# Clustered attention and a SoLU layer on one core: paired x transposes, row placements without mutual waits, and a new written order

## The chip, the cores and the metric

The kernel runs on one core of one Trainium2 chip. The core has five engines that run their own instruction streams and meet at semaphores: TensorE (PE; its weight loads are listed apart as PEld), VectorE (DVE), ScalarE (ACT), GpSimd (POOL) and SyncE (SP), which here does nothing but issue DMAs. The metric is the device time of one execution in microseconds (us), lower is better. "Span" is the time from the first to the last instruction of a profiled execution.

## What is computed

Two parts, one after the other. The first is attention restricted to clusters: each query and each key is assigned to the nearest of 16 centroids of its head, and a query sees only keys of its own cluster. The second is a feed-forward layer with a SoLU activation (h times softmax of h) and a layer norm, over rows of 512 that hold all 8 heads of a token.

```
batch, n_heads, seq, head_dim = 4, 8, 768, 64        # n_clusters = 16
q_assign = argmax(q_n . c_n)                         # q_n, k_n, c_n: rows of unit length
k_assign = argmax(k_n . c_n)
scores = where(q_assign == k_assign, q . k / sqrt(64), -1e9)
attn   = softmax(scores) @ v
x      = attn.transpose(0, 2, 1, 3).reshape(3072, 512)
h      = x @ w_in                                    # 512 x 1024
solu   = h * softmax(h)
ln     = (solu - mean) / sqrt(var + 1e-6) * g_ln     # over the 1024
out    = ln @ w_out                                  # 1024 x 512, float32
```

## The kernel before

**Attention.** The work goes by batch b (0 to 3) and pair p of heads (0 to 3). Queries and keys of a pair are loaded (`ld`, four DMAs of 96 KB for each of q and k in batches 1 to 3), turned so that the head dimension lies on the partitions (`xt` on VectorE; in batch 0 `tp` on TensorE and a copy `xa`), and cast to bf16 into a tile `qk` (`ca`). For each token the products with the centroids are made (`cl`, TensorE), transposed back (`tb`), reduced to their maximum (`mx`), compared with it into a one-hot row (`oh`), and turned again (`ot`), all on VectorE. These one-hot rows are then placed below the casted rows of the `qk` tile (`pl`, line 450), for queries and keys (i = 0, 1) and for the first and second half of the columns (part = 0, 1): four placements for a pair, by VectorE, GpSimd or a DMA of SyncE. `bl` zeroes some rows. One matmul over the casted rows and the one-hot rows together (`S`, line 535) gives the score plus a large bias where the clusters agree; the exponential (`E`, ScalarE, line 541) takes the bias off again. The exponentials are the weights of the matmuls with v (`V`, line 558; v is loaded by `lv` and cast by `cv`), whose last column is the sum for the softmax. `N` (lines 570 and 583, VectorE) divides by it and writes x in bf16.

Scores go by units; a group of units shares one accumulator bank, so that the first `V` of a group waits for `N` of the group before. In batches 0 to 2 the units of the last head pair are grouped by two token blocks: blocks 2s and 2s+1 of both heads end in one `N`. In batch 3 the heads 4 to 7 are done one token block at a time.

**Feed-forward.** It goes by token blocks f of 128 rows (24 of them, six per batch). `tx` (lines 600 to 604) turns x of a block by a transposing DMA into a buffer `xT`, of which there are four. `h` (line 634) are four steps of two matmuls into two of three banks; `hm` the maximum (640), `ex` the exponential (646), `u` the product (651); `tu` (656) turns u by a DMA; `bn` and `ag` the statistics; `at` and `al` the scale factor on GpSimd; `y` (692) the second matmul, four steps of two; `sc` (700 on ScalarE, 702 on VectorE) the scaling; `ou` (712) the store. The last blocks' `tx` and `tu` are done by TensorE instead.

**The order.** The program's class `Weave` holds, for each of the five engines, a written order: a text of kinds with counts ("ld4 lv si ld7 ...") that is expanded, kind by kind, into the operations in the order in which they were added. `AWAY` lists the operations that run on another engine than their first choice. `add` declares each operation with its estimated cost, the operations that it needs, and those that it must come after. From this the program computes start times with a model and emits the instructions in that order; on the chip each engine runs its own stream in the written order, and waits at semaphores that the framework derives from the tiles each instruction reads and writes. An operation that must wait holds up all that follow it on its engine; for SyncE that is every load, transpose, placement and store behind it.

Operations are named by kind and indices: `tx6` is the x transpose of block 6, `ld3.3.1` the load of the keys of pair 3 in batch 3 (its fourth part), `pl2.3.0.1` the placement of the second half of the query rows of pair 3 in batch 2.

The dependence of two placements on each other comes from the framework: they write different columns of the same rows of one `qk` tile, and where they run on different engines, the later one waits for the earlier.

Of the kernel before, what the change touches and what calls it, by code (L numbers as in the profile page):

```python
# [10 lines left out]
F32 = mybir.dt.float32  # L11
# [11 lines left out]
class Weave:  # L23
# [6 lines left out]
        ld4 lv si ld7 lg ld lv ld8 lo3 lv ld4 lo lv ld4 li ld li2 ld5 li ld3 tx ld3 lv tx ld9 tx tu  # L30
        lv ld tx ld3 tx tu ld2 tx lv ld4 pl ld4 lv ld4 lv ld4 ou lv tu2 ld4 tx ld2 ou ld tx2 ld2 tu2
        ou ld tx ld7 tx lv ld4 ou2 tu ld2 pl ld3 tu ld2 lv ld tx lv pl ld pl ou ld2 lv ld2 tu pl tu
        ld2 pl ou tx ld3 tx pl2 ld tx ld ou tx2 lv tu2 tx lv ou tu ou pl ou pl2 ou tu2 tx ou tu tx2
        tu2 ou2 tx tu tx ou tu ou2 tu2 ou6
    """
    ORDER["POOL"] = """
        po z2 ca2 pl ca bl cv ca pl cv pl bl pl2 z ca z pl ca2 pl2 ca2 pl cv2 ca2 pl2 sg ca2 bl cv
        pl cv pl3 ca2 bl cv wi2 pl2 bl wi pl wi pl ca3 pl2 bl pl cv ca z ca3 pl ca cv at2 ca cv pl2
        ca2 pl2 bl al cv2 ca al at pl bl at pl2 cv2 ca6 at al cv pl cv pl3 at cv ca2 bl al2 pl2 ca3
        pl2 ca bl at ca pl al ca4 pl2 al cv2 ca2 bl at ca pl2 cv at al cv bl al ca2 pl at bl pl ca  # L40
        cv at2 cv ca pl al pl2 al2 bl cv pl4 at ca cv at cv al at3 al3 at2 al at al at al at al at
        al at al3
    """
    ORDER["PE"] = """
        tp cp tp2 cl tp cl tp2 S3 tp2 S tp2 S2 cl S3 tp2 S V2 S V tp S cl V2 S V S tp gt S3 tp S4 V
        S V2 S5 V2 S V tp S3 cl S2 V2 S2 V S V3 S5 V3 S V S3 V2 S4 me S3 V3 S V2 S V S3 cl S V S2 V
        S V2 S2 V2 S5 V4 S3 cl S2 V2 S2 V2 S3 V2 S h S h S3 h2 S V S2 V cl S2 h S V4 h V S V S2 h S2
        h V S2 V2 S cl V S h S V2 S h y S3 h S h V2 S V S h S y2 S3 V h y V S2 V S h2 S2 V4 S V S2 V
        S h y2 h S2 y S2 V2 S V S y S V S V S h2 V S2 h2 cl S3 V2 S V4 S3 h2 S3 cl S V4 S3 y3 V S3
        V3 S y S2 h3 V S V2 S3 V y S h S2 y S2 V S y2 S V4 h2 S V S2 cl S h V h S2 V2 S y S2 y V3 S3  # L50
        h y2 h S2 h2 S h V S2 h y3 V S V y S V S V2 S y2 S y V2 S3 V2 h S y S2 V S V h S cl S3 V2 h
        V S cl V S2 h S2 cl S2 V2 S2 h S h2 S V3 S2 V2 y S2 y V y2 S2 h V2 S V S V S y S2 V2 S2 h V
        h S V S2 y S2 y2 S V h2 S2 V3 S cl S3 h2 S V2 S V2 S2 V2 h cl S3 h3 S y V y3 S V S V S h S h
        V2 S V S h S2 h S V2 h S V y S2 y V y S h S y V S2 V S h2 V h S2 y S2 y S y V y V4 S2 h2 S2
        h y S V h V3 y S y S2 y S h V S3 V3 h2 S V h S2 y V y3 S2 h V S V h2 S y3 S y S h S h y V2
        h2 S3 h S V2 y3 S2 V2 h3 V S V y3 h y S3 h y h2 y3 h2 S y4 S h2 V4 y3 ptx y h2 y h2 y3 ptu2
        y4 ptu2 y8
    """
    ORDER["DVE"] = """
        cn cb ca xa tb mx oh ot pl2 tb pl mx oh xa3 ot pl xa pl tb mx oh ot tb N bl xa xt gk mx oh  # L60
        ot su2 xa2 N su cv ca su2 tb N su ca2 mx su2 oh ot N xt ce xt N ce2 tb mx oh N ot ce xt N
        ce4 N tb mx oh ot xt2 hm cv N tb u xt N xt hm mx bn tb u oh N ot bn hm mx oh xt u ot N ag bn
        hm sc bn2 N ag u xt bn xt2 hm bn N u tb N mx ag oh hm ot tb N bn xt u bn N mx xt bn ag cv oh
        N ot ag hm xt bn2 u ag ca N tb mx xt hm ca bn N u oh xt ot hm xt2 u ca N bn2 ag bn3 ca xt N
        hm tb mx oh ot tb u xt ag mx N bn oh tb cv2 ot ag hm mx N sc u N oh xt bn hm ot N bn xt sc u
        N bn bl tb hm xt ag bn u tb N hm mx2 oh u ot oh N sc hm bn ag bn ag bn cv ot u N hm bn2 ca
        bn u bl ag N hm N bn u N sc hm bn2 ag2 u bn ag hm N bn u bn2 hm N u bn2 ag2 hm N bn u bn2 ag
        hm sc bn ag u ag bn hm N tx u bn ag bn hm sc bn u ag tu2 bn2 ag
    """
    ORDER["ACT"] = """  # L70
        wa xa2 ca2 xa2 ca E ca E4 xa E4 xa2 E19 xa E58 ex E10 ex E11 ex E9 ex E9 sc E5 ex E11 ex E8
        sc E10 ex E2 sc E9 ex E5 sc E ex E3 sc E8 sc E6 ex E8 ca E8 ex E12 ex E11 ex E3 ca2 E3 ex
        E10 ex E4 sc E6 ex E sc E6 ex E9 ex E3 sc E2 ex sc E5 ex E4 sc E ex sc E2 ex E3 sc ex sc ex
        sc tu2 sc2
# [3 lines left out]
        ca0.0.0.0.0 ca0.0.0.1.1 ca3.1.0.1 ca3.3.0.0 ca3.3.0.1 tu23.1 xa0.0.0.0 xa0.1.0.0 xa0.2.0.1  # L78
        xa0.2.1.0 xa0.2.1.1 xa0.3.1.1
    """.split(), "ACT"))  # L80
    AWAY.update(dict.fromkeys("""
        bl0.1 bl3.1 bl3.3 ca0.0.1.0.0 ca0.3.0.0 ca0.3.1.0 ca1.0.0.0 ca2.2.0.0 ca2.3.0.1 ca3.0.0.0
        ca3.0.0.1 ca3.3.1.1 cv0.1.0 cv1.0.1 cv2.0.1 cv2.3.1 cv3.0.0 cv3.2.1 pl0.0.0.0.1 pl0.0.0.1.1
        pl0.0.1.1.1 sc0 sc12 sc17 sc20 sc7 sc8 sc9 tu22.0
    """.split(), "DVE"))
    AWAY.update(dict.fromkeys("""
        ca0.0.1.0.1 pl0.0.0.1.0 pl0.0.1.1.0 pl0.1.0.0 pl0.1.0.1 pl0.1.1.0 pl0.1.1.1 pl0.2.0.0
        pl0.2.0.1 pl0.2.1.0 pl0.2.1.1 pl0.3.0.0 pl0.3.0.1 pl0.3.1.0 pl0.3.1.1 pl1.0.0.0 pl1.0.0.1
        pl1.0.1.0 pl1.0.1.1 pl1.1.0.0 pl1.1.0.1 pl1.1.1.0 pl1.1.1.1 pl1.2.0.0 pl1.2.0.1 pl1.2.1.0
        pl1.2.1.1 pl1.3.0.0 pl1.3.0.1 pl1.3.1.1 pl2.0.0.0 pl2.0.0.1 pl2.0.1.0 pl2.0.1.1 pl2.1.0.0  # L90
        pl2.1.0.1 pl2.1.1.0 pl2.1.1.1 pl2.2.0.0 pl2.2.0.1 pl2.2.1.1 pl2.3.0.1 pl2.3.1.1 pl3.0.0.0
        pl3.0.0.1 pl3.1.0.0 pl3.1.0.1 pl3.2.0.0 pl3.2.0.1 pl3.2.1.0 pl3.3.1.0 pl3.3.1.1
# [79 lines left out]
def kernel(  # L172
# [276 lines left out]

    def place(b, p, hf, i, part, e):  # L450

        n = asg[b, p, hf, "n"]
        r = slice((2 * i + part) * NB, (2 * i + part + 1) * NB)
        lo = (hf or 0) * HALF + part * n
        dst = side(b, p, i, slice(0, 2), slice(lo, lo + n))[D:D + NB]
        src = asg[b, p, hf, "oht"][r, :n]
        if e == "SP":
            nc.sync.dma_start(out=dst, in_=src.unsqueeze(1).to_broadcast([NB, 2, n]))
        else:
            VEC[e].tensor_copy(dst.bitcast(F32), src.bitcast(F32).unsqueeze(1)  # L460
                               .to_broadcast([NB, 2, n // 2]))
# [137 lines left out]

    def turn_x(f):  # L600
        b, su = divmod(f, n_t)
        xTs[f] = mo.tile([P, n_dc, P], BF16, name="xT", bufs=4)
        nc.sync.dma_start_transpose(out=xTs[f][:],
                                    in_=xs[b][:, su].rearrange("p h d -> p (h d)"))

    def turn_x_pe(f):
        b, su = divmod(f, n_t)
        xTs[f] = mo.tile([P, n_dc, P], BF16, name="xT", bufs=4)
# [5 lines left out]
    def keep_x(f):  # L614
        nc.vector.tensor_copy(xTs[f][:], ff[f, "xp"][:])
# [313 lines left out]
    for g, ns in enumerate(GROUPS):  # L929
# [14 lines left out]
        if b >= 2:  # L944
            nd += [f"tx{(b - 2) * n_t + s2}" for s2 in range(n_t)]
# [15 lines left out]
    for f in range(n_f):  # L961
# [5 lines left out]
        prev = s  # L967
    for f in range(n_f):
        s = pos[f] - 8 * (f == n_f - 1)
        b, su = divmod(f, n_t)  # L970
        gs = sorted({group_of[where[b, h, su]] for h in range(H)})
        nd = [f"N{g2}" for g2 in gs]
        if f >= 4:
            nd.append(f"h{f - 4}.1.1")
        if f"tx{f}" in turns:
# [122 lines left out]
```

## Time and profile before

| what | value |
|---|---|
| median of 3 runs | 243.21 us (242.08 to 243.49) |
| the profiled execution | 242.2 us, of which the span is 240.3 us |
| mean granted TensorE clock | 0.997 |
| DMA | 39.13 MB in 134158 packets, mean 163 GB/s |
| DMAs issued by SyncE, by kind | 96 loads of 96 KB after batch 0, 23 x transposes, 22 u transposes, 24 stores, 11 placements, 16 loads of v |

The profile lists, for each engine, its busy time and its instructions in order of time; where an engine sat idle, the brackets behind a row give the idle time just before it and what ended it. Several instructions of one line that follow each other are merged into one row with their count. "SPq" rows are DMA issues of SyncE; their duration is the time that SyncE spent on issuing. A tile view gives the shortest, median and longest duration of the instructions that write or read a tile.

### The profile page before, as it was taken

What the parts mean: (1) busy time and instruction counts of PE and PEld (TensorE: products, weight loads), DVE (VectorE), ACT (ScalarE), POOL (GpSimd) and SP (SyncE); (2) the same over time, 40 slices, a digit from 0 to 9 for tenths busy, and PEclk for the clock granted to TensorE, in tenths of its full rate; (3) what the DMA queues carried; (4) which work ended last, traced back from release to release, by engine and by line L of the source; (5) the groups of instructions that cost most, each with busy time, mean ns of one, the idle gap of its engine ahead of it and who ended that gap; (6) DMA issues with size and microseconds to landing.
All of it is one profiled execution on the core that took longest, in us unless ns stands there. A gap on an engine that the chain in (4) does not pass through costs nothing.

```text
span 240.3 us, 6552 instructions
## 1 busy us (share of the span) xinstructions
PE 220.1 (92%) x2380; PEld 146.3 (61%) x2380; DVE 201.6 (84%) x359; ACT 196.2 (82%) x378; POOL 125.0 (52%) x234
## 2 busy tenths in 40 slices
PE   2999898999999989899996999897999999999983
PEld 1555575576767757576664666664676776665541
DVE  3885999999899969969959999678898778899880
ACT  3597998999899989978977999786999988885442
POOL 2446699899547778749184555242049204033130
PEclk9999999999999999999999999999999999999998
DMA  6999889979898989989889959757991523747522
GB/s 160 263 240 247 209 210 257 197 114 190 143 177 171 154 190 212 146 170 164 135 213 170 163 141 163 160 93 142 210 170 64 131 56 81 195 91 209 141 86 89
DMA packets 134158, 39.13 MB, mean 163 GB/s; under 512 B 124712, under 2 KB 129520, under 8 KB 134128
## 3 DMA queue, kind: packets, MB, share of 16 engines
q1 hardware_dynamic: 132528, 38.34, 77.6%
q10 hardware_dynamic: 1600, 0.39, 0.7%
q8 instruction: 18, 0.29, 0.5%
q14 instruction: 12, 0.10, 0.1%
HBM read 23.11 MB, written 6.29 MB: 122 GB/s over the span
## 4 chain that ended last, share of the span: by engine, by line
PE 55%; DVE 15%; DMA 14%; SPq 6%; issue 4%; ACT 4%; POOL 0%; DVEq 0%; ACTq 0%; POOLq 0%
PE sps L535 16%; PE yps L692 13%; PE hreg L634 13%; PE ops L558 9%; DMA uT<-u 6%; DMA raw<-in_q_dram 3%; SPq L358 3%; PE csc L415 3%; ACT e L541 3%; DVE nmax L640 2%; DVE w_sum L513 2%; DMA vf<-in_v_dram 2%; SPq L378 2%; DMA raw<-in_k_dram 2%; DVE xt L386 2%
## 5 line engine op out<-in xcount | busy, mean ns | idle before, releaser
L541 ACT ACTIVATE e<-sps 128x512 bf16<-128x512 f32 (+1 forms) x294 | 152.1, 600 | 18.7 <-PE sps L535 17.0
L535 PE MATMUL sps<-qk 80*128 80x256 bf16 (+5 forms) x636 | 97.3, 264 | 2.2 <-ACT e L541 0.4
L535 PEld LDWEIGHTS <-qk 96*128 96x128 bf16 (+1 forms) x636 | 60.6, 121 | 32.1 <-issue 13.6
L558 PEld LDWEIGHTS <-e 128*128 128x128 bf16 x1152 | 51.0, 97 | 13.5 <-issue 4.9
L558 PE MATMUL ops<-v,e 128*128 128x65 bf16 x1152 | 55.3, 193 | 1.9 <-DVE x L583 1.3
L634 PE MATMUL hreg<-w_in_sb,xT 128*128 128x512 bf16 x192 | 52.9, 379 | 1.1 <-DMA xT<-x 1.0
L692 PE MATMUL yps<-w_out_c,uT 128*128 128x512 bf16 x184 | 48.9, 379 | 4.3 <-DMA uT<-u 3.6
L460 POOL COPY qk<-oht 32x384 f32<-32x384 f32 (+1 forms) x52 | 27.9, 536 | 25.9 <-DVE oht L448 19.4
L646 ACT ACTIVATE e_sb<-hreg,nmax 128x1024 bf16<-128x1024 f32 x24 | 26.8, 1116 | 9.6 <-DVE nmax L640 9.5
L640 DVE TENSOR_REDUCE nmax<-hreg 128x1 f32<-128x1024 f32 x24 | 29.0, 1207 | 4.6 <-PE hreg L634 4.4
L662 DVE BATCH_NORM_STATS2 bs<-u 128x6 f32<-128x512 bf16 x48 | 31.4, 673 | 0.0
L678 POOL TENSOR_SCALAR esq<-es,mv 128x1 f32<-128x1 f32 x24 | 9.1, 378 | 41.7 <-DVE mv L666 39.3
L386 DVE STREAM_TRANSPOSE xt<-raw 128x768 f32<-128x768 f32 x24 | 23.3, 969 | 8.5 <-DMA raw<-in_q_dram 3.7
L651 DVE TENSOR_TENSOR u<-e_sb,hreg 128x1024 bf16<-128x1024 bf16 x24 | 28.9, 1202 | 1.4 <-ACT e_sb L646 1.0
L692 PEld LDWEIGHTS <-uT 128*128 128x128 bf16 x192 | 17.2, 97 | 17.8 <-DMA uT<-u 4.3
L406 POOL TENSOR_SCALAR qk<-xt 64x768 bf16<-64x768 f32 (+1 forms) x29 | 24.6, 848 | 2.2 <-DVE xt L386 0.4
L634 PEld LDWEIGHTS <-xT 128*128 128x128 bf16 x192 | 17.0, 97 | 9.9 <-DMA xT<-x 1.3
L404 POOL CAST qk<-xt 64x768 bf16<-64x768 f32 (+1 forms) x23 | 19.7, 856 | 5.7 <-DVE xt L372 4.7
L583 DVE TENSOR_TENSOR x<-ops,den 128x384 bf16<-128x384 f32 (+1 forms) x37 | 18.6, 504 | 1.3
L474 POOL CAST v<-vf 128x384 bf16<-128x384 f32 x26 | 14.2, 553 | 8.0 <-DMA vf<-in_v_dram 7.3
L415 PE MATMUL csc<-xt,c_bd 128*32 128x384 f32 (+1 forms) x136 | 16.6, 501 | 1.4 <-DVE xt L386 1.3
L700 ACT ACTIVATE y<-yps,alpha 128x512 f32<-128x512 f32 x16 | 11.2, 701 | 4.8 <-PE yps L692 1.7
(69 smaller groups left out, 159.3 us busy)
## 6 DMA issues: line engine op xcount, KB each, us to landing
vf<-in_v_dram SPq DMA_DIRECT2D x16, 384.0 KB, 4.5
out_dram<-y SPq DMA_DIRECT2D x24, 256.0 KB, 2.3
raw<-in_q_dram SPq DMA_DIRECT2D x50, 96.0 KB, 3.4
raw<-in_k_dram SPq DMA_DIRECT2D x50, 96.0 KB, 3.2
w_g<-in_moe_w_out_dram SPq DMA_DIRECT2D x4, 512.0 KB, 5.7
w_st<-in_moe_w_in_dram SPq DMA_DIRECT2D x4, 512.0 KB, 5.1
raw<-in_q_dram SPq DMA_DIRECT2D x6, 192.0 KB, 4.0
raw<-in_k_dram SPq DMA_DIRECT2D x6, 192.0 KB, 4.4
```

Source lines behind the costliest of these rows:

```text
L386: nc.vector.transpose(xt[:], raws[b, p, i][:].rearrange("p j c -> p (j c)"))
L406: VEC[e].tensor_scalar(dst, xt[r, cols], scalar1=inv_C, scalar2=1.0, op0=Alu.mult, op1=Alu.mult)
L460: VEC[e].tensor_copy(dst.bitcast(F32), src.bitcast(F32).unsqueeze(1) .to_broadcast([NB, 2, n // 2]))
L535: nc.tensor.matmul(sps_[n, k][:, c0:c0 + w], side(b, h // 2, 1, h % 2, keys)[r], side(b, h // 2, 0, h % 2, slice(s0 * P, s0 * P + w))[r])
L541: nc.scalar.activation(es[n, k][:, :w], sps_[n, k][:, :w], Act.Exp, scale=exp_scale, bias=-exp_scale)
L558: nc.tensor.matmul(opss[g][:, s, :VW], es[n, k][:, c0:c0 + P], v1[slot(b, h // 2)][:, h % 2, kt, :VW], start=(kt == 0), stop=(kt == n_t - 1))
L634: uses(nc.tensor.matmul(hreg[:, at(f, f2)[1], :], xTs[f][:, dc, :], w_in_sb[:, dc, f2 * FF2:(f2 + 1) * FF2], start=(dc == 0), stop=(dc == ...
L640: uses(nc.vector.tensor_reduce(ff[f, "nmax"][:], pair_of(f), axis=AXY, op=Alu.max, negate=True), *both(f))
L646: uses(nc.scalar.activation(ff[f, "e"][:], pair_of(f), Act.Exp, bias=ff[f, "nmax"][:], accum_out=ff[f, "esum"][:]), *both(f))
L651: uses(nc.vector.tensor_tensor(ff[f, "u"][:], ff[f, "e"][:], pair_of(f), op=Alu.mult), *both(f))
L662: nc.vector.bn_stats(ff[f, "bs"][:, f2, :], ff[f, "u"][:, f2, :])
L692: ins = nc.tensor.matmul(ff[f, "y"], ff[f, "uT"][:, at(f, f2)[0] * (n_fc // 2) + c, :], w_out_c[:, fc, :], start=(fc == 0), stop=(fc == n_ ...
```

## The change

Four things change.

1. `turn_x` takes two token blocks with one DMA in batches 0 to 2 (f below 18): blocks 2s and 2s+1 go as one transpose of 128 by 1024 into a buffer for two blocks, of which there are three. In batch 3 it stays one block at a time, in a buffer of the same size. Nine of the 23 transposing DMAs of x disappear, and the `h` steps of both blocks wait for the one DMA.
2. `place` declares to the framework that two placements into the same tile side, if they are on different engines, do not depend on each other ("other columns").
3. The planner gets further needs (`reader`): steps of block f that reuse a small buffer name the step of block f - 4 that reads it. They emit no instruction.
4. The five written orders and the lists in `AWAY` are new. By the lists, 66 operations change their engine; among them two copies `xa`, some casts, zeroings and scalings go to VectorE, and eight placements instead of 11 are DMAs of SyncE.

```
     def place(b, p, hf, i, part, e):
...
         if e == "SP":
-            nc.sync.dma_start(out=dst, in_=src.unsqueeze(1).to_broadcast([NB, 2, n]))
+            ins = nc.sync.dma_start(out=dst, in_=src.unsqueeze(1).to_broadcast([NB, 2, n]))
         else:
-            VEC[e].tensor_copy(dst.bitcast(F32), src.bitcast(F32).unsqueeze(1)
-                               .to_broadcast([NB, 2, n // 2]))
+            ins = VEC[e].tensor_copy(dst.bitcast(F32), src.bitcast(F32).unsqueeze(1)
+                                     .to_broadcast([NB, 2, n // 2]))
+        for other in placed.get((b, p, hf, i), []):
+            if other.ins.engine != ins.ins.engine:
+                tc.declare_no_dep(ins.ins, other.ins, reason="other columns")
+        placed.setdefault((b, p, hf, i), []).append(ins)
...
+    def turned(f):
+        return list(range(f - f % 2, f - f % 2 + 2)) if f < (B - 1) * n_t else [f]
+
+    def take_x(f):
+        fs = turned(f)
+        xT = mo.tile([P, 2, n_dc, P], BF16, name="xT", bufs=3)
+        for j, f1 in enumerate(fs):
+            xTs[f1] = xT[:, j]
+        return xT[:, :len(fs)].rearrange("p s c t -> p (s c) t")
+
     def turn_x(f):
         b, su = divmod(f, n_t)
-        xTs[f] = mo.tile([P, n_dc, P], BF16, name="xT", bufs=4)
-        nc.sync.dma_start_transpose(out=xTs[f][:],
-                                    in_=xs[b][:, su].rearrange("p h d -> p (h d)"))
+        nc.sync.dma_start_transpose(out=take_x(f), in_=xs[b][:, su:su + len(turned(f))]
+                                    .rearrange("p s h d -> p (s h d)"))
...
+    def reader(kind, f):
+        return [f"{kind}{f - 4}"] if f >= 4 else []
...
-            add(f"tx{f}", "SP", 1.28, s, (lambda e, f=f: turn_x(f)), nd,
-                [f"tx{f - 1}"] if f else [], move=0.75, lag=(0.1, 0.7))
...
+                add(f"tx{f}", "SP", 1.28, s, (lambda e, f=f: turn_x(f)), nd,
+                    [f"tx{x_turns[-1]}"] if x_turns else [], move=0.65 * len(fs), lag=(0.1, 0.7))
...
-                nd = [f"tx{f}"] + [f"wi{dc}" for dc in range(n_dc)]
+                nd = [f"tx{fs[0]}"] + [f"wi{dc}" for dc in range(n_dc)]
...
-                [f"u{f}"], [f"bn{f}.0"] if f2 else [])
-        add(f"ag{f}", "DVE", 0.13, s + 8, (lambda e, f=f: f_aggr(f)), [f"bn{f}.0", f"bn{f}.1"])
...
+                [f"u{f}"] + reader("ag", f), [f"bn{f}.0"] if f2 else [])
+        add(f"ag{f}", "DVE", 0.13, s + 8, (lambda e, f=f: f_aggr(f)),
+            [f"bn{f}.0", f"bn{f}.1"] + reader("al", f))
```

The part of SyncE's order that the prediction speaks of, before (first) and after, with the operations' names, around the transpose of block 6 and on to the last load of batch 3:

```
ld2.3.0.0 ld2.3.0.1 ld2.3.0.2 tx6 ld2.3.0 ld2.3.1.0 ou1 ld2.3.1.1 tx7 tx8 ld2.3.1.2 ld2.3.1 tu4 tu5
ou2 ld3.0.0.0 tx9 ld3.0.0.1 ld3.0.0.2 ld3.0.0 ld3.0.1.0 ld3.0.1.1 ld3.0.1.2 ld3.0.1 tx10 lv2.2
ld3.1.0.0 ld3.1.0.1 ld3.1.0.2 ld3.1.0 ou3 ou4 tu6 ld3.1.1.0 ld3.1.1.1 pl2.2.1.0 ld3.1.1.2 ld3.1.1
ld3.2.0.0 tu7 ld3.2.0.1 ld3.2.0.2 lv2.3 ld3.2.0 tx11 lv3.0 pl2.3.1.0 ld3.2.1.0 pl2.3.0.0 ou5
ld3.2.1.1 ld3.2.1.2 lv3.1 ld3.2.1 ld3.3.0.0 tu8 pl3.0.1.0 tu9 ld3.3.0.1 ld3.3.0.2 pl3.0.1.1 ou6 tx12
ld3.3.0 ld3.3.1.0 ld3.3.1.1 tx13 pl3.1.1.0 pl3.1.1.1 ld3.3.1.2 tx14 ld3.3.1

ou1 ld2.3.0.0 ld2.3.0.1 tx6 tu3 ld2.3.0.2 ld2.3.0 ld2.3.1.0 tu4 tu5 tx8 ou2 ld2.3.1.1 ld2.3.1.2
ld2.3.1 ld3.0.0.0 ld3.0.0.1 ld3.0.0.2 lv2.2 tu6 ld3.0.0 ou3 ld3.0.1.0 ld3.0.1.1 ld3.0.1.2 ld3.0.1
pl2.2.1.1 tx10 lv2.3 ld3.1.0.0 ld3.1.0.1 pl2.2.0.0 ld3.1.0.2 ld3.1.0 ld3.1.1.0 ld3.1.1.1 ou4
ld3.1.1.2 ld3.1.1 ld3.2.0.0 ld3.2.0.1 ld3.2.0.2 ld3.2.0 ld3.2.1.0 tu7 lv3.0 lv3.1 ou5 ou6 ld3.2.1.1
ld3.2.1.2 ld3.2.1 ld3.3.0.0 ld3.3.0.1 ld3.3.0.2 tu8 ld3.3.0 lv3.2 ld3.3.1.0 ld3.3.1.1 ld3.3.1.2 tx12
ld3.3.1
```

124 lines of the change are left out of this document (65 added, 59 removed).

## The prediction

> **What bounds the kernel now.** I read the page's busy shares first, then the busy time of each engine in stretches of 20 us, then the idle time of TensorE in order of time, and last SyncE's issues just ahead of each idle piece.
>
> ```profile
> span 240.3 us, 6552 instructions
> PE 220.1 (92%) x2380; PEld 146.3 (61%) x2380; DVE 201.6 (84%) x359; ACT 196.2 (82%) x378; POOL 125.0 (52%) x234
> ```
> ```profile
> 0.00:20.00 20.00, 14.83 (x123) 8.83 (x124) 12.90 (x40) 11.43 (x26) 8.84 (x27) 1.00 0.93 216
> 20.00:40.00 20.00, 17.96 (x195) 11.61 (x194) 18.44 (x33) 18.20 (x40) 15.85 (x20) 1.00 0.89 225
> 40.00:60.00 20.00, 19.19 (x252) 13.42 (x251) 19.34 (x35) 19.30 (x37) 18.16 (x29) 1.00 0.93 186
> 60.00:80.00 20.00, 19.55 (x246) 14.69 (x245) 18.93 (x30) 18.59 (x37) 11.82 (x22) 1.00 0.94 164
> 80.00:100.00 20.00, 19.20 (x226) 13.45 (x224) 17.72 (x32) 18.72 (x38) 15.76 (x30) 1.00 1.03 179
> 180.00:200.00 20.00, 20.00 (x248) 14.25 (x247) 15.95 (x28) 17.96 (x35) 7.92 (x19) 1.00 0.39 93
> ```
>
> The columns of the second fence are the stretch, its length, then PE, PEld, DVE, ACT and POOL busy, the granted clock, the DMA share and GB/s. TensorE is the bound: from 180 to 200 us it has no idle time at all. So only TensorE's idle time ahead of that can be won. From 20 to 80 us VectorE has almost none either (1.56, 0.66 and 1.07 us, 3.29 us in all); ScalarE is close behind. The DMA engines are at 0.89 to 1.03 up to 100 us.
>
> The idle pieces of TensorE between 86 and 170 us are these:
>
> ```profile
> 90.20 0.54 PE L558 MATMUL ops<-v,e 128*128 128x65 bf16 x12 [0.80 <-DVE x L583]
> 101.73 1.47 PE L634 MATMUL hreg<-w_in_sb,xT 128*128 128x512 bf16 x6 [1.04 <-DMA xT<-x]
> 128.06 1.04 PE L692 MATMUL yps<-w_out_c,uT 128*128 128x512 bf16 x4 [2.44 <-DMA uT<-u]
> 150.84 0.61 PE L692 MATMUL yps<-w_out_c,uT 128*128 128x512 bf16 x2 [1.11 <-DMA uT<-u]
> 166.34 0.84 PE L415 MATMUL csc<-xt,c_bd 128*32 128x384 f32 x4 [1.28 <-DVE xt L386]
> ```
>
> In brackets stand the idle time and what ended it. The last four, 5.87 us together, belong by the written order to h6, y6, y8 and cl3.3, and all four wait for something that SyncE issued. SyncE's own queue tells why it came late:
>
> ```profile
> L378 SPq DMA_DIRECT2D raw<-in_q_dram x48: 336/526/3358, 15.6 to 155.2; - x48
> ```
> ```profile
> 98.92 1.20 SPq L603 DMA_TRANSPOSE xT<-x  x1
> 118.79 4.68 SPq L378 DMA_DIRECT2D raw<-in_q_dram  x4
> 123.57 0.94 SPq L712 DMA_DIRECT2D out_dram<-y  x2
> 124.62 1.29 SPq L656 DMA_TRANSPOSE uT<-u  x1
> 137.60 0.62 SPq L458 DMA_DIRECT2D qk<-oht  x1
> 141.15 0.59 SPq L458 DMA_DIRECT2D qk<-oht  x1
> 145.26 3.82 SPq L656 DMA_TRANSPOSE uT<-u  x1
> 157.00 2.39 SPq L603 DMA_TRANSPOSE xT<-x  x1
> 162.76 0.59 SPq L378 DMA_DIRECT2D raw<-in_k_dram  x1
> ```
> ```profile
> 96.06 0.18 DVE L570 RECIPROCAL den<-ops 128x4 f32<-128x4 f32 x1 [0.31 <-PE ops L558]
> 96.27 0.42 DVE L583 TENSOR_TENSOR x<-ops,den 128x256 bf16<-128x256 f32 x1
> 140.06 1.06 POOL L460 COPY qk<-oht 32x384 f32<-32x384 f32 x2 [4.04 <-DMA qk<-oht]
> ```
>
> The first row gives the shortest, median and longest issue of a load in ns. In the others the columns are start, duration, engine and line. The x of block 6 was complete at 96.69 (the normalising step), but its transpose was issued at 98.92, behind two loads. The transpose tu6 stands behind four loads and the stores ou3 and ou4 and issues at 124.62; y6 follows it. A row placement at 137.60 holds GpSimd for 4.04 us, and those GpSimd copies in turn hold the next placement to 141.15: halves of one tile waiting for each other, with tu8 behind them. The last load, ld3.3.1 at 162.76, stands behind the transposes tx12 to tx14 and was what cl3.3 waited for.
>
> **The change part by part.** *One transpose for two blocks.* Nine of 23 x transposes go. The nearest row for the double one is uT, whose 128 by 1024 bf16 is the pair's shape exactly:
>
> ```profile
> L603 SPq DMA_TRANSPOSE xT<-x x23: 1189/1258/2551, 50.0 to 214.1; - x23
> DMA to landing us min/median/max: 2.4/3.0/5.1
> L656 SPq DMA_TRANSPOSE uT<-u x22: 1232/1277/3824, 63.4 to 221.6; - x22
> DMA to landing us min/median/max: 3.0/3.3/6.4
> ```
>
> SyncE is freed of 9 x 1.258 = 11.3 us of issuing, less 9 x 0.02 us for the larger one, spread over the first three batches, from 50 us on; the landing of the first block of a pair comes 0.3 us later. Bytes moved are the same. A pair could have to wait for its second block, but here doesn't: in batches 0 to 2 the last head pair is normalised for blocks 2s and 2s+1 in one step, so both become ready together. Three buffers of two blocks hold no less than four of one. On TensorE's path itself: nothing; the worth is in what SyncE issues earlier.
>
> *Placements without waiting.* This takes away waits like the 4.04 us on GpSimd and the one that ended at 141.15. No instruction goes. Neither is on TensorE's path by itself; the gain is already in y8 below. At worst it is nothing.
>
> *The planner's "reader" edges* add no instruction and no wait on the chip: they only constrain how the order is built.
>
> *The new order.* I expanded both written orders by operation and compared places. The work between two places I count in TensorE time at these rates:
>
> ```profile
> 183.40 0.44 PE sps L535 x4
> 186.57 0.75 PE ops L558 x24
> 187.79 0.86 PE hreg L634 x4
> ```
>
> For h6: tx6 has one load less straight ahead, and by the median issue times it comes some 5 us of issuing earlier in SyncE's order, so that it waits only for its own x. From the last value matmul it needs to h6 lie 4.5 us of TensorE work in both orders; it needs normalising (96.06 to 96.69 here, with the hop some 0.7 us) and 3.3 us to land, 4.0 us: gone. For y6: tu6 now stands ahead of ou3, ou4 and most of the ld3.0 and all ld3.1 loads, with 24 us of TensorE work between y2 (the last store ahead of it is ou2) and y6: gone. For y8: tu8 has only ou6 ahead, 19 us before y8, and both pl2.3 placements of the second part are on GpSimd: gone. For cl3.3: ld3.3.1 is passed by one transpose only, not three, and stands right behind tx12, whose x is ready some 6 us of TensorE work before h12: gone. So 5.87 us are removed. The 0.80 us at 90.20 I leave as it is.
>
> What does SyncE's new order hold up instead? tu3 now stands behind tx6, which blocks the queue until its x is ready. From there to y3 lie 13 pairs of score matmuls, 30 value matmuls and 16 matmuls of the two layers: 26 x 0.11 + 30 x 0.031 + 16 x 0.215 = 7.2 us; needed are 0.7 + 1.26 + 3.3 = 5.3 us, so it is hidden with 1.9 us to spare; without that cover it costs what is missing. I find no worse place, but the present order let four SyncE stalls through as well. New stalls are between 0 and the same 5.87 us; I take one as large as the largest there is, 2.44 us, since SyncE has 11.3 us more room.
>
> *Work moved between engines.* To the end of batch 1, VectorE gets a net two turned-token copies, two half casts, two zeroings and one output scaling; full casts and v casts that come and go cancel, and two short placements that leave it I don't count.
>
> ```profile
> L372 DVE COPY xt<-hreg 128x384 f32<-128x384 f32 x8 | 4.2, 548 | 0.1
> 7.07 0.35 DVE L406 TENSOR_SCALAR qk<-xt 64x384 bf16<-64x384 f32 x1 [0.69 <-ACT xt L372]
> L465 DVE MEMSET qk<- 16x384 f32 x3 | 1.1, 378 | 0.9 <-DMA qk<-oht 0.7
> L702 DVE TENSOR_SCALAR y<-yps,alpha 128x512 f32<-128x512 f32 x7 | 5.2, 741 | 0.4
> ```
>
> That is 2 x 0.548 + 2 x 0.35 + 2 x 0.378 + 0.741 = 3.3 us. The casts and one copy lie in the first 20 us, where VectorE has 7.1 us idle; one copy, the zeroings and the scaling, 2.0 us, come later, against 3.29 us of idle time. A loss is between 0 and 3.3 us, and I take a third of the later ones, 0.7. In the start, the first turned copy moves to VectorE and the second key transpose goes ahead of the centroids' one, which attacks the 0.69 us that VectorE waits for ScalarE's copy: a gain of 0 to 0.69, taken as 0.4. On the other side the two copies leave ScalarE, which is nearly full at 20 to 60 us; that stays uncounted.
>
> *Sum:* -5.87 - 0.4 + 2.44 + 0.7 = -3.1 us. The profiled execution took 242.2 us (its span 240.3 and 1.9 around it) and would become 239.1; the median of the runs, 243.2, lies 1.0 higher, so 240.1 us.
>
> **Rivals.** *VectorE becomes the bound* (slower). The added 3.3 us meet 3.29 us of idle time from 20 to 80 us. If the early idle time can't take them, because it consists of waits for data, each normalising step up to about 85 us comes up to 3.3 us later; value matmuls need it for their bank, as the 0.80 us row shows, and x transposes block SyncE for as long, so that the old stalls come back in other places. Then 243.2 + 3.3 - 0.4 = 246.1 us. It decides from the point where the work ahead of a normalising step grows by more than VectorE's idle time before it. For it: 19.34 of 20 us busy. Against: counted over the written order, the work ahead of u6 (the product at about 110 us) grows by only some 0.3 us, since other steps move behind it, so it would be a passing delay. Chance 0.15.
>
> *The transfers bind, not their issue* (no change). With the DMA share at 0.89 to 1.03, an earlier issue only queues longer; the four loads at 118.79 took 4.68 us to issue where the median is 0.526 each, which speaks for it. Against: the waits behind stores, placements and unready x aren't transfers. Only the start is gained: 242.8 us. Chance 0.17.
>
> *VectorE's casts hold up GpSimd* (within 1%).
>
> ```profile
> L460 POOL COPY qk<-oht x52: 343/503/1191, 9.9 to 183.2; 32x384 f32<-32x384 f32 x49, 32x192 f32<-32x192 f32 x3
> L460 POOL COPY qk<-oht x11: 498/503/507, 39.6 to 57.3; 32x384 f32<-32x384 f32 x11
> ```
>
> The first row is the whole span, the second 40 to 60 us. In batches 0 and 1 VectorE has nine casts and zeroings more and five fewer, net four; if each stretches one GpSimd copy from 503 to 1191 ns, GpSimd loses 2.8 us where it is busy for 18.16 of 20, and the forecast becomes 242.9 us. Against: in just that stretch all eleven copies took 498 to 507 ns. Chance 0.05. [...]
>
> *All is won*, without new stalls and with ScalarE's relief: under 236.9 (243.2 - 5.87 - 0.4). Chance 0.05.
>
> **How the numbers follow.** The forecast, the removed stalls less one new one, has 0.58 and runs from 236.9 (nothing given back) to 242.9; I put 0.48 of it below 240.8 and 0.10 above. One per cent, 2.4 us, is about what a measurement of this kernel can tell from no change. Faster: 0.48 + 0.05 = 0.53. Within 1%: 0.10 + 0.17 + 0.05 = 0.32. Slower: 0.15. The range goes from 236.9 to 245.5; below lies 0.05, above most of the slower case, 0.13.
>
> **What would show it.** Right: nine x transposes fewer, each pair landing in about 3.3 us; no idle TensorE at h6, y6, y8 and cl3.3; no GpSimd wait on a placement's DMA for copies; at most some 3 us of new idle pieces. Wrong: value matmuls waiting on the normalising step between 25 and 85 us (VectorE), loads and transposes that land later after issue while SyncE waits less (transfers), or GpSimd copies well over 503 ns.

## The result, and the profile after

| kernel | median (lowest to highest) | ratio to before, 95% interval |
|---|---|---|
| before | 243.35 us (242.08 to 246.94, 4 runs) | |
| after | 232.62 us (232.27 to 232.70, 4 runs) | 0.957 [0.953, 0.961] |

Each ratio, here and below, leaves out the runs in a slower state of the chip, while the medians take them in, so a quotient of two medians can differ from the ratio.

The change is worth 4.3%, more than the range that was forecast allowed. The profiled execution of after took 232.3 us, with a span of 230.3 us, 10.0 us less than the span of before.

The page of after, span and busy time of each engine:

```profile
span 230.3 us, 6548 instructions
PE 217.0 (94%) x2380; PEld 146.8 (64%) x2380; DVE 204.7 (89%) x363; ACT 194.2 (84%) x375; POOL 123.6 (54%) x236
```

Next the busy time in stretches, with the columns of the prediction: after from 0 to 100 us, and the middle part, 60 to 180 us, as one stretch; then that middle stretch of before.

```profile
0.00:20.00 20.00, 16.23 (x127) 10.03 (x128) 15.49 (x43) 12.48 (x28) 8.43 (x24) 1.00 0.93 228
20.00:40.00 20.00, 17.21 (x206) 11.37 (x204) 19.42 (x36) 17.32 (x37) 16.29 (x26) 1.00 1.00 223
40.00:60.00 20.00, 18.40 (x242) 12.39 (x241) 18.65 (x32) 18.78 (x38) 14.62 (x24) 1.00 0.89 185
60.00:80.00 20.00, 20.00 (x250) 15.34 (x247) 19.26 (x32) 19.37 (x38) 12.46 (x22) 1.00 1.03 182
80.00:100.00 20.00, 19.81 (x237) 14.32 (x236) 19.79 (x36) 19.33 (x39) 14.64 (x28) 1.00 0.84 181
...
60.00:180.00 120.00, 119.81 (x1387) 85.86 (x1384) 111.38 (x188) 114.25 (x219) 72.86 (x135) 1.00 0.86 167
```
```profile
60.00:180.00 120.00, 112.50 (x1270) 78.22 (x1269) 104.74 (x178) 105.77 (x203) 63.38 (x116) 1.00 0.90 165
```

The first busy figure of a row is TensorE's. Between 60 and 180 us its idle time falls from 7.50 us (120 less 112.50) to 0.19. Before 60 us nothing is won: busy for 51.98 us there before (the three rows in the prediction), 51.84 after. After 180 us the idle time is 0.3 us more. The remaining part of the 10 us is a fall of TensorE's own busy time, 220.1 to 217.0, which the section on the prediction comes back to.

All of after's idle pieces of TensorE from 15 to 190 us that the timeline names:

```profile
33.03 0.55 PE L564 MATMUL ops<-v,e 128*128 128x65 bf16 x12 [1.32 <-DVE x L589]
38.05 0.35 PE L564 MATMUL ops<-v,e 128*128 128x65 bf16 x6 [0.58 <-DVE xt L386]
48.37 0.55 PE L564 MATMUL ops<-v,e 128*128 128x65 bf16 x12 [1.01 <-DVE x L589]
90.78 1.04 PE L650 MATMUL hreg<-w_in_sb,xT 128*128 128x512 bf16 x4 [0.19 <-DVE u L667]
```

None is ended by a DMA any more. The paired transposes, from the tile view of `xT`, and SyncE's queue around the steps that were late before:

```profile
L619 SPq DMA_TRANSPOSE xT<-x x14: 1190/1270/2688, 50.4 to 204.2; - x14
...
DMA to landing us min/median/max: 2.4/3.3/4.9
```
```profile
109.97 1.24 SPq L672 DMA_TRANSPOSE uT<-u  x1
...
126.00 3.79 SPq L378 DMA_DIRECT2D raw<-in_q_dram  x4
...
140.32 1.31 SPq L672 DMA_TRANSPOSE uT<-u  x1
...
145.25 1.67 SPq L619 DMA_TRANSPOSE xT<-x  x1
146.97 0.57 SPq L378 DMA_DIRECT2D raw<-in_k_dram  x1
```

The first row takes in the five single transposes of batch 3. The nine pairs alone took SyncE 1.287 us each (median), against 1.255 for the 18 single ones in whose place they stand, so a pair costs SyncE what a single one cost; it lands after 3.7 us instead of 3.0. `tu6` goes out at 109.97 instead of 124.62, `tu8` at 140.32 instead of 145.26, and the last load of all, `ld3.3.1`, at 146.97 instead of 162.76, 15.8 us earlier. Four loads still take 3.79 us to issue at 126.00, but no named idle piece of TensorE is ended by them. No GpSimd copy waits for a placement's DMA any more, as the prediction said.

### The profile page after: what moved, and what is told of

Its sections match the earlier page's. It is cut to its first block, busy times and chain, and to the rows that moved or that the text cites. A ratio compares the mean times of both kernels' runs of the same rounds, so it can differ in the third digit from the quotient of the medians.

```text
span 230.3 us, 6548 instructions
## 1 busy us (share of the span) xinstructions
PE 217.0 (94%) x2380; PEld 146.8 (64%) x2380; DVE 204.7 (89%) x363; ACT 194.2 (84%) x375; POOL 123.6 (54%) x236
## 4 chain that ended last, share of the span: by engine, by line
PE 72%; DVE 15%; DMA 4%; issue 3%; POOL 2%; ACT 2%; SPq 1%; DVEq 0%; ACTq 0%; POOLq 0%
PE sps L541 21%; PE hreg L650 16%; PE yps L708 16%; PE ops L564 12%; PE csc L415 4%; PE hreg L365 2%; DVE xt L386 2%; DMA w_st<-in_moe_w_in_dram 2%; DVE w_sum L519 2%; DMA vf<-in_v_dram 1%; DVE nmax L656 1%; DVE oh L442 1%; ACT e L547 1%; POOL qk L462 1%; DVE bs L678 1%
## 5 line engine op out<-in xcount | busy, mean ns | idle before, releaser
L462 POOL COPY qk<-oht 32x384 f32<-32x384 f32 (+1 forms) x57 | 30.9, 541 | 39.0 <-DVE oht L448 27.3
L694 POOL TENSOR_SCALAR esq<-es,mv 128x1 f32<-128x1 f32 x24 | 8.2, 344 | 39.3 <-DVE mv L682 22.1
L406 POOL TENSOR_SCALAR qk<-xt 64x768 bf16<-64x768 f32 x28 | 23.5, 840 | 5.8 <-DVE xt L386 3.9
L386 DVE STREAM_TRANSPOSE xt<-raw 128x768 f32<-128x768 f32 x24 | 22.6, 954 | 0.0
L404 POOL CAST qk<-xt 64x768 bf16<-64x768 f32 (+1 forms) x22 | 18.4, 834 | 1.0
L415 PE MATMUL csc<-xt,c_bd 128*32 128x384 f32 (+1 forms) x136 | 16.0, 502 | 0.1
L716 ACT ACTIVATE y<-yps,alpha 128x512 f32<-128x512 f32 x15 | 10.4, 693 | 5.5 <-PE yps L708 2.7
```

Source lines behind the costliest of these rows:

```text
L386: nc.vector.transpose(xt[:], raws[b, p, i][:].rearrange("p j c -> p (j c)"))
L415: nc.tensor.matmul(csc[c * NB:(c + 1) * NB, :n], c_bd[:, p, :], xts[b, p, i][:, lo + part * n:lo + (part + 1) * n], tile_position=(0, c * NB))
L462: ins = VEC[e].tensor_copy(dst.bitcast(F32), src.bitcast(F32).unsqueeze(1) .to_broadcast([NB, 2, n // 2]))
```

## The experiments

The theories: **A**, the new written order carries the gain; **B**, the pairing does, because SyncE issues one thing after another and everything behind nine issues comes earlier; **D**, the placements' waits do; **E**, the pair's buffers give the x transposes more room; **F**, a pair is cheaper as a transfer than two single ones, whoever issues it. Where an expectation names another letter, it says there what is meant.

All results, each ratio against the kernel before on the same chip (its median beside it). The rows come from three chips: `after_old_sync_order` and the three with `v_on_gpsimd` from a second, the last two rows from a third. The kernel before moved by up to 1 us on one and the same chip (240.95 to 242.02), so differences of under 1% between rows with different values of "before" say little.

| run | median us | before us | ratio, 95% interval |
|---|---|---|---|
| pairs_in_old_order | 237.67 | 242.02 | 0.981 [0.972, 0.990] |
| no_waits_in_old_order | 238.88 | 242.02 | 0.988 [0.980, 0.997] |
| both_in_old_order | 233.95 | 241.44 | 0.973 [0.967, 0.979] |
| new_order_alone | 239.28 | 241.44 | 0.994 [0.990, 0.999] |
| unpaired | 238.77 | 241.44 | 0.992 [0.989, 0.996] |
| placements_wait | 232.18 | 241.44 | 0.966 [0.957, 0.975] |
| six_buffers | 242.32 | 242.02 | 1.001 [0.996, 1.006] |
| tiny_loads | 235.89 | 242.02 | 0.974 [0.968, 0.981] |
| before_v_on_gpsimd | 244.42 | 241.65 | 1.014 [1.005, 1.023] |
| unpaired_v_on_gpsimd | 241.86 | 241.65 | none |
| after_v_on_gpsimd | 237.76 | 241.65 | 0.986 [0.977, 0.995] |
| after_old_sync_order | 242.86 | 241.65 | 1.007 [1.003, 1.012] |
| sync_pause | 238.07 | 240.95 | 0.990 [0.985, 0.994] |
| before_fewer_v | 232.25 | 240.95 | 0.968 [0.961, 0.975] |
| unpaired_fewer_v | 234.63 | 240.95 | 0.978 [0.970, 0.985] |
| changed_again | 231.83 | 240.95 | 0.967 [0.959, 0.975] |
| after_fewer_v | 234.31 | 241.96 | 0.966 [0.956, 0.975] |
| new_sync_order_old_rest | 256.07 | 241.96 | 1.054 [1.043, 1.066] |

`unpaired_v_on_gpsimd` has no ratio, and nothing below rests on it.

### Which part of the change

**One code change each, in the old order.** `pairs_in_old_order` takes only the pairing, and strikes the second transpose of each pair from SyncE's list; `no_waits_in_old_order` takes only the declaration in `place`.

```
-        ... si ld3 tx ld3 lv tx ld9 tx tu lv ld tx ...
+        ... si ld3 tx ld3 lv ld9 tx tu lv ld4 ...
```

> The kernel before with one change: pairs of x blocks turned by one DMA (three buffers of two), the odd x transposes struck out of the order, placements waiting as before. B (each transpose fewer moves all behind it in SyncE's full queue forward): 233 to 235 us. D (the missing waits of the placements did it in the run with both code changes): 238 us or more.

> The kernel before with one change: placements don't wait for each other; x turned singly, four buffers, old orders. B: 240 to 243 us, as before within 1%. D: 234 to 238 us.

**Both code changes in the old order, and the new order without either.** The second one has single transposes, six `xT` buffers and the waits.

> The code changes alone (pairs, no mutual waits of placements), in the five orders of the kernel before, with the nine odd x transposes struck out. Theory A (the places in SyncE's written order make the gain): the loads and u transposes stand behind the same steps as before, so little is won: 240 to 243 us. Theory B (nine transposes fewer free SyncE and the DMA engines): most of the gain is here: 233 to 236 us. Theory C (the orders of the compute engines and the moves between engines make it): 241 to 243 us, as A.

> The five new orders and the new AWAY lists alone: two single x transposes stand where the pair stood (buffers for six blocks as in the changed kernel), placements wait for each other. A: 233 to 235 us, since two issues in one place hold SyncE only 1.26 us longer. B: 239 to 243 us. C: 233 to 235 us, as A.

The two code changes without any new order already give 2.7%, and the new order without them 0.6%. A falls. One at a time in the old order, the pairing gives 1.9% and the missing waits 1.2%, which add up to a little more than the 2.7% of both together. So D has a share there. Both single runs, 237.67 and 238.88 us, came out between the ranges of B and of D, since neither expected that the gain would be divided.

**One code change taken out of the changed kernel.** `unpaired` has two single transposes where a pair was, and six buffers of one block; `placements_wait` has only the declaration removed.

```
     def turned(f):
-        return list(range(f - f % 2, f - f % 2 + 2)) if f < (B - 1) * n_t else [f]
+        return [f]
...
-        for other in placed.get((b, p, hf, i), []):
-            if other.ins.engine != ins.ins.engine:
-                tc.declare_no_dep(ins.ins, other.ins, reason="other columns")
-        placed.setdefault((b, p, hf, i), []).append(ins)
```

> The changed kernel with two single x transposes in the place of each pair, all else kept. A and C: 232.5 to 234.5 us. B: 237 us or more.

> The changed kernel without the declaration, so that placements of one tile side on different engines wait for each other again. A, B and C: 232.5 to 233.5 us, since in the new order the halves seldom meet in time. A rival D, that the missing waits make the gain (in the kernel before one such chain held SyncE for some 2.3 us ahead of tu8, and GpSimd for 4.0): 235 us or more, with idle TensorE again behind SyncE between 140 and 155 us.

Without the pairing most of the gain is gone: 238.77 against 232.18 for its companion on the same chip, 6.6 us. The waits of the placements cost nothing that shows in the new order. So the same 1.2% that the missing waits give in the old order is covered by the rest of the change. The longer idle pieces of TensorE in `unpaired` after 60 us:

```profile
64.58 0.60 PE L653 MATMUL hreg<-w_in_sb,xT 128*128 128x512 bf16 x2 [0.68 <-DMA xT<-x]
82.94 0.61 PE L711 MATMUL yps<-w_out_c,uT 128*128 128x512 bf16 x2 [1.16 <-DMA uT<-u]
...
130.47 0.40 PE L544 MATMUL sps<-qk 80*128 80x256 bf16 x2 [2.49 <-DMA raw<-in_q_dram]
```

Only the first waits for an x transpose. The others wait for a transpose of u and for a load, which stand behind x transposes on SyncE, as B has it. Its last load goes out at 154.18 us, 7.2 us later than in after.

### Why the pairing gains

**More room, no pairing** (E): the kernel before with six `xT` buffers instead of four.

> The kernel before with x buffers for six blocks instead of four, all else kept; the pairs bring this with them. Buffers theory E (the room, not the fewer DMAs): 234 to 237 us. B: 240 to 243 us, as before.

No change. E falls.

**Small loads that only cost issuing.** The changed kernel with three loads of 128 bytes, which nobody reads, behind each paired transpose.

```
+        for j in range(3 if len(turned(f)) == 2 else 0):
+            c = slice(4 * (f // 2 * 3 + j), 4 * (f // 2 * 3 + j) + 4)
+            nc.sync.dma_start(out=g_rows[:, c], in_=moe_g_ln.rearrange("(a p) -> a p", p=P)[:, c])
```

> The changed kernel with three loads of 128 bytes behind each paired transpose on SyncE (27 in all), which cost SyncE some 0.4 us each and move next to nothing: about the SyncE time of the nine transposes that went. B, by SyncE's time: 237 to 240 us, as unpaired (238.8). Rival F, that a transposing DMA costs the transfers themselves: 232 to 234 us.

They took 0.293 us each (median) and 9.6 us in all, since the first of each three takes some 0.47. From the end of a pair to the next issue of the changed kernel it is 11.6 us over the nine places in place of 1.1, so SyncE is held for 10.5 us. The time rose to 235.89, by 4.1 us against the changed kernel on the same chip (`changed_again`, 231.83). That lies between the two ranges: it speaks for B, at a lower price than expected, but 27 DMAs more could also cost something as transfers.

**SyncE held without any transfer.** The changed kernel with 20 empty drain instructions on SyncE behind each pair.

```
         nc.sync.dma_start_transpose(out=take_x(f), in_=xs[b][:, su:su + len(turned(f))]
                                     .rearrange("p s h d -> p (s h d)"))
+        if len(turned(f)) == 2:
+            for j in range(20):
+                nc.sync.drain()
```

> The changed kernel with 20 empty drain instructions on SyncE behind each of the nine paired transposes: SyncE is held and no transfer is added, and no row and no packet of the paired transposes changes. By the theory that SyncE's time is what the pairing buys (B), the time rises by about half of the time that the drains add: if one takes 0.06 us, 9 x 1.2 = 11 us of SyncE and 237 to 239.5; if they turn out shorter, in proportion (3 us of SyncE would give 234). By the rival that a pair is cheaper as a transfer (F), the pause costs nothing: 232 to 233.5.

> The changed kernel as it is, on the chip of the three others, so that they can be read against it: 231.5 to 233.5 by every theory.

SyncE's queue in the two, first `sync_pause`, then after:

```profile
60.79 1.26 SPq L619 DMA_TRANSPOSE xT<-x  x1
63.55 0.41 SPq L475 DMA_DIRECT2D vf<-in_v_dram  x1
64.06 1.24 SPq L619 DMA_TRANSPOSE xT<-x  x1
66.76 0.88 SPq L378 DMA_DIRECT2D raw<-in_q_dram  x2
```
```profile
59.36 1.25 SPq L619 DMA_TRANSPOSE xT<-x  x1
61.12 0.40 SPq L475 DMA_DIRECT2D vf<-in_v_dram  x1
61.63 1.25 SPq L619 DMA_TRANSPOSE xT<-x  x1
62.93 1.60 SPq L378 DMA_DIRECT2D raw<-in_q_dram  x2
```

From the end of the transpose to the next issue it is 1.50 and 1.46 us in place of 0.51 and 0.05. Added up over the nine places the gaps are 14.7 us against 1.1, so the drains hold SyncE for 13.6 us. No byte and no DMA was added, and yet 6.2 us of the gain are lost (238.07 against 231.83), nearly what taking the pairs apart costs. F can't explain that. TensorE waits at two of the three places of `unpaired`, in `sync_pause` at:

```profile
65.50 0.60 PE L653 MATMUL hreg<-w_in_sb,xT 128*128 128x512 bf16 x2 [1.18 <-DMA xT<-x]
129.47 0.60 PE L541 MATMUL sps<-qk 80*128 80x256 bf16 x2 [2.47 <-DMA raw<-in_k_dram]
```

A share for F beside B isn't excluded by this: at the price of the drains, 6.2 us for 13.6, the 11.3 us of the nine transposes would cost 5.1 of the 6.6 us of `unpaired`. So F is looked for where it would show, in the time that the transfers take. The largest queue in the pages' DMA section, with its packets, MB and the time of its packets as a share of the 16 DMA engines over the span, first `unpaired`, then after:

```profile
q1 hardware_dynamic: 132288, 38.20, 74.6%
```
```profile
q1 hardware_dynamic: 132000, 38.19, 78.5%
```

That is 177 us of 237.6 with single transposes and 181 us of 230.3 with pairs: in the new order the single transposes took the DMA engines no more time than the pairs. In the old order it is 186.5 us before and 181.8 in `pairs_in_old_order`, so a share for F stays open there.

**SyncE freed, transposes single.** In the next three runs the 15 later loads of v are left out; the first pair's v stands in for all, so the result is that of another v. The median load cost SyncE 0.526 us.

```
+        if (b, p) != (0, 0):
+            vfs[b, p] = vfs[0, 0]
+            return
         vf = vp.tile([P, 2, n_t, D], F32, name="vf")
```

> The kernel before without the 15 later loads of v: the first pair's v stands in for all of them, and the casts stay. SyncE loses some 15 x 0.5 = 7.5 us of issuing, and nothing takes them over, neither GpSimd nor another queue. B: 237 to 239.5. F (the single transposes cost what they cost as transfers): 241 to 243.

> The changed kernel with two single transposes for each pair, and without the 15 later loads of v (the first pair's stand in). B: 7.5 of the 11.3 us that unpairing costs SyncE come back, 234 to 236.5. F: 238 to 239.5, as unpaired.

> The changed kernel without the 15 later loads of v (the first pair's stand in), so that SyncE is freed of another 7.5 us. It tells how much SyncE's issuing still costs the changed kernel. By B with the full queue already relieved (TensorE is idle for 0.2 us between 60 and 180 us): 230.5 to 232, 1.3 us or less below the changed kernel. If every microsecond of SyncE were still worth half a microsecond, as it was in the unpaired kernel: 228 to 229.

In the kernel before, with its 23 single transposes, its old order and its waits, this alone gives 3.2%, as much as the whole change on that chip (3.3%), and 8.7 us by the medians, far more than B's range of 237 to 239.5 allowed. Its middle stretch and the idle piece of TensorE in it:

```profile
60.00:180.00 120.00, 119.46 (x1347) 83.82 (x1344) 111.03 (x189) 112.78 (x216) 69.16 (x129) 1.00 0.75 130
```
```profile
156.44 0.84 PE L415 MATMUL csc<-xt,c_bd 128*32 128x384 f32 x4 [0.41 <-DVE xt L386]
```

TensorE is idle for 0.54 us where it was idle for 7.50. Of the four late steps of the prediction h6, y6 and y8 no longer wait, and cl3.3 waits for 0.41 us instead of 1.28, without one of them being moved. The gain is so large because more than the v loads' own time went: added up over the trace, SyncE's issues took 181.8 us in the kernel before and 160.3 here, 8.6 less for v, 9.3 less for the 112 loads of q and k (83.2 to 73.9) and 4.2 less for the 23 transposes of x. So 21.5 us were freed, not 7.5, and the 8.7 us are again 0.4 for each. `unpaired_fewer_v` gets back 4.1 us of what unpairing cost (238.77 to 234.63), where B had 234 to 236.5; SyncE's issues went from 176.6 to 163.4 us there, which is 0.3 for each. These runs also carry less data (DMA share 0.75 instead of 0.90), and the issues that got shorter are most likely an effect of that, so by themselves they leave open what the transfers cost; only `sync_pause` changes no data. In the changed kernel the same relief gives nothing that a comparison across chips can show (0.966 against 0.967 and 0.957): what SyncE cost there is used up, as far as 1% can tell.

**The v loads on another queue.** The same 15 loads issued by GpSimd, in the kernel before, in `unpaired` and in the changed kernel.

```
+        eng = nc.gpsimd if (b, p) != (0, 0) else nc.sync
-        nc.sync.dma_start(out=vf[:].rearrange("p h t d -> p h (t d)"),
+        eng.dma_start(out=vf[:].rearrange("p h t d -> p h (t d)"),
```

> The kernel before with the 15 later loads of v issued by GpSimd's queue instead of SyncE's; every transpose stays single, no order and no wait is changed. By the theory that SyncE's serial issuing is what the pairing relieves (B), some 15 x 0.5 = 7.5 us of issuing leave SyncE and the time falls by 2 to 4 us, to 238 to 240. By the rival that the transposes themselves cost less when paired (F: their transfers, lanes or packets), nothing about them is changed, and the time stays at 241 to 243.

> The changed kernel with two single transposes for each pair (the earlier run of it alone: 238.8) and the 15 later loads of v on GpSimd's queue. B: SyncE gets back 7.5 of the 11.3 us that unpairing costs it, 235 to 236.5. F: the single transposes still cost what they cost, 238 to 239.5.

> The changed kernel with the 15 later loads of v on GpSimd's queue. B: TensorE is idle for only 0.2 us between 60 and 180 us, so what SyncE gives up now has little left to buy: 231.5 to 233.5. If the issuing costs GpSimd's own copies time that somebody waits for, 233 to 235.

This went wrong for both theories: the kernel before became 1.4% slower, and the changed kernel gains only 1.4% over it (0.986) in place of 3.3 or more. The tile view of `vf` in `before_v_on_gpsimd`:

```profile
L470 POOL DMA_DIRECT2D vf<-in_v_dram x15: 769/785/944, 9.0 to 169.9; - x15
...
L470 SPq DMA_DIRECT2D vf<-in_v_dram x1: 487/487/487, 3.4 to 3.4; - x1
```

An issue costs GpSimd 0.785 us (the median of 15); SyncE's 16 in the kernel before have a median of 0.526. So 11.8 us went to an engine whose copies others wait for. The run moves the cost instead of removing it, and so decides nothing between B and F.

### What the order is worth

Two mixes: the changed kernel with SyncE's old order (pairs kept), and its mirror, both code changes with SyncE's new order and the old orders of the four other engines.

> The changed kernel with SyncE's old written order (pairs kept; GpSimd's, ScalarE's, VectorE's and TensorE's orders stay new). By the theory that the new order of SyncE carries the gain (A), 235 to 238. By B the pairs are what matters, and the order is worth about what it was worth on top of both code changes, 1 per cent or less: 233 to 234.5.

> Both changes of code and SyncE's new order, with the old orders of the four other engines: the mirror of the run with SyncE's old order and the others' new ones (242.9). If SyncE's new order is good by itself (A), it is no slower than both changes of code in the old orders, 232 to 234.5. If the order of SyncE only has to fit the orders of the engines that it feeds, a mix is slower whichever half is old: 236 to 243.

Both are slow, 242.86 and 256.07 us, while the old orders together give 233.95 and the new ones together 232. The first is outside the ranges of A and B alike. Neither mix is pure: which placements are SyncE's follows from the lists of the other engines, so some stand in its order at places chosen for the mix, four in the mirror. SyncE's longest wait in the mirror, and two idle pieces of TensorE in it:

```profile
SPq L462 <- DVE oh L444: 13.6, 1, 13.6
```
```profile
131.88 0.74 PE L566 MATMUL ops<-v,e 128*128 128x65 bf16 x12 [4.51 <-DVE x L591]
...
176.31 1.49 PE L417 MATMUL csc<-xt,c_bd 128*32 128x384 f32 x4 [5.88 <-DVE cst L426]
```

In the first row stand the total, the count and the longest wait in us: SyncE stood for 13.6 us, from 173.7 to 187.3, before a placement whose one-hot rows VectorE makes later in that mix, with transposes and stores queued behind it; the loads of q and k were out by then. The four added placements held it for another 4.0 and 3.8 us, at 137 and 145 us. TensorE's two pieces are ended by VectorE's steps; how they follow from SyncE's waits isn't shown. So the mixes say nothing for or against the new order of SyncE by itself; they only show that orders not made for each other can cost more than the whole change brings. What the new order adds to both code changes is 0.6 to 1.6% (0.967 and 0.957 against 0.973); in the first case the intervals overlap, and the second takes its two ratios against two different values of before.

No run beat the changed kernel beyond its interval.

## Why the prediction was wrong

The direction was right (0.53 for faster) and the time was outside the range: 240.1 forecast, 236.9 to 245.5, and 232.6 measured.

**The step that failed** is the price of the pairing: "On TensorE's path itself: nothing; the worth is in what SyncE issues earlier." The mechanism in its second half was right, and 11.3 us of freed issuing was right as well (nine issues fewer, at nearly the same duration each). But no term of the sum took it in; it served only as a reason to take 2.44 and not 5.87 for new stalls. The runs price it at 4.4 us in the old order (237.67 against 242.02) and 6.6 in the new one. All that was removed was credited to the new order instead, step by step for h6, y6, y8 and cl3.3, and the order alone brings 0.6%: in `new_order_alone` TensorE waits elsewhere, for 0.90 us at 66, 1.58 at 84 and 2.25 at 128 us. The views had shown it: behind each of the four late steps stood a SyncE row that came late because of the rows before it.

In the terms of the sum, the span fell by 10.0 us where 3.1 were forecast. Of the 6.9 us between, 3.9 lie in the stalls between 60 and 180 us (7.31 us less, for 5.87 less 2.44) and 3.1 in TensorE's busy time, which the sum held constant; the start and the end make up the rest.

**The sum's -5.87** was taken from the four largest idle pieces; the stretch from 60 to 180 us held 7.50 us, and 7.31 of it went. The 0.80 us piece "left as it is" went too. The 3.1 us of busy time are not faster matmuls: added up one by one, the durations of the 2380 matmuls are 625.3 us before and 626.8 after. Busy time is the time that at least one matmul covers, and matmuls overlap; by the profile, which models their ends, it fell because they follow each other more closely. So the prediction's "only TensorE's idle time ahead of that can be won" was too narrow: there was something to win inside the busy time as well, where no row names a wait. What the matmuls waited for there isn't shown.

**The +2.44 for a new stall** didn't come; the only piece between 60 and 180 us is 0.19. For the order alone it was no bad guess, as the three pieces of `new_order_alone` show. That the order before "let four SyncE stalls through" was no ground for expecting another with the pairing: the four were one shortage of SyncE's time, as `before_fewer_v` shows, and it was gone. `tu3` behind `tx6` shows in no idle piece, as counted.

**+0.7 for VectorE and -0.4 for the start**, +0.3 together, came out as +0.14 (51.98 less 51.84). Both have something in them: value matmuls now wait for the normalising step for 1.32 and 1.01 us at 33 and 48 us, where the prediction's rival expected it, and the start before 20 us is 1.4 us better (14.83 to 16.23 busy). The rival itself, all of the extra work on the path up to 85 us and the old stalls coming back, didn't come.

**"Transfers bind"** was wrong: a full DMA share of 0.89 to 1.03 hid no gain, and the share is hardly lower after (0.84 to 1.03 up to 100 us). Something of it is left: where less data is carried, in `before_fewer_v`, the issues of the other loads get shorter (83.2 to 73.9 us for the 112 loads of q and k). "VectorE's casts hold up GpSimd" showed nothing: GpSimd's placing copies took 502 ns (median) after, 876 at most, against 503 and 1191 before.

**Placements without waiting, "at worst nothing"**, held: nothing in the new order, 1.2% in the old.

**"All is won"**, at under 236.9, was the case that came, with a chance of 0.05. Its own sum, 5.87 and 0.4 us off, ends at 236.9, still 4.3 us above the result, since it too priced neither the pairing nor the busy time.

## What to carry over

A queue that issues in order is a resource like an engine, though no busy table lists it: where several late steps have rows of one queue behind them, add up what the change takes off that queue and price it at the stalls in all of its followers, not only at the transfer itself. Here a us of SyncE's time was worth 0.4 to 0.6 us (11.3 us for 4.4 in the old order and 6.6 in the new, 13.6 us of drains for 6.2, 10.5 us of small loads for 4.1), and nothing that could be measured once TensorE had next to no idle time left. An issue moved to another engine is charged there (0.785 us for a load of v on GpSimd, 0.526 on SyncE), and an order that is written for one engine belongs to the orders written with it. An engine's busy share also doesn't say how closely its instructions are packed: compare the sum of their durations with the time that they cover (here 625.3 us in 220.1 before and 626.8 in 217.0 after).

## What the runs showed of the hardware

**A stall can cost more than its own row.** After the 2.49 us of idle time in `unpaired`, TensorE's granted clock (the column before the last two) fell to 0.50, and four score matmuls took 1.04 us there where four took 0.60 later:

```profile
128.00:130.00 2.00, 0.00 (x0) 0.00 (x0) 1.57 (x3) 0.73 (x2) 1.91 (x3) 1.00 1.21 206
130.00:132.00 2.00, 1.40 (x14) 1.08 (x16) 0.92 (x1) 0.17 (x1) 1.87 (x3) 0.71 0.97 212
132.00:134.00 2.00, 2.00 (x18) 1.31 (x16) 0.06 (x1) 1.51 (x3) 0.87 (x2) 0.50 0.98 176
134.00:136.00 2.00, 2.00 (x25) 1.40 (x27) 1.20 (x3) 1.53 (x3) 0.00 (x0) 0.94 1.05 170
```
```profile
132.09 1.04 PE L544 MATMUL sps<-qk 80*128 80x256 bf16 x4
...
135.23 0.60 PE L544 MATMUL sps<-qk 80*128 80x256 bf16 x4
```

The lost share of the clock, (0.29 + 0.50 + 0.06) x 2 us, is 1.7 us on top of 2.49. The same follows the stall of 2.47 us in `sync_pause`, with 0.84, 0.50 and 0.80 from 128 to 134 us. The stall of 2.44 us in the kernel before, at 128.06, was followed by a clock of 1.00 from 128 to 136 us. A lower clock also came with shorter pieces: in `changed_again` it was 0.91 over the stretch from 20 to 40 us, where the longest piece that the timeline names is 1.15 us (at 32.05), and six score matmuls took 1.47 us there at 34.74 where six took 1.06 at 27.39. In after, with 1.32 us at the same step, the clock was 1.00 over the same stretch. So the length of an idle piece alone doesn't tell in these runs whether the clock falls behind it: 2.44 us went without a fall, and a stretch whose longest named piece is 1.15 us had one. What decides it isn't shown.

**An empty instruction has its price.** The 180 drains held SyncE for 13.6 us, 0.08 us each. The nine gaps are 1.46 to 1.97 us long, with nothing to wait for that the profile shows.

**An issue's length isn't fixed.** The 112 loads of q and k took SyncE 83.2 us to issue in the kernel before and 73.9 without the 15 loads of v; the difference lies in the long ones: 26 issues over 0.7 us took 37.8 us in the first, 16 took 22.0 in the second. That less traffic is the reason is the nearest reading; it isn't shown by itself.
